# K's tail weights first, a later second output projection, an earlier last w2 piece and earlier weight sums in a pre-LN attention and MLP kernel

## The chip, the cores and the metric

The kernel runs on one core of one Trainium2 chip. The metric is the time of one execution on the device, in microseconds (us). Before the change the median of three runs was 367.53 us (367.42 to 367.68).

The engines are named as in the profile: PE is TensorE, DVE is VectorE, ACT is ScalarE, POOL is GpSimd, and SP is the engine that issues most transfers. "Before" and "after" are the two kernels.

## The reference

One pre-LN transformer block on x of shape (1, 2048, 576), bf16. There are 32 heads of 18 channels. Each position looks at 8 positions, itself and seven earlier ones at distances of 2.

```python
def _A_ref(x, wqkv, wo):                       # sliding, dilated attention
    qkv = (x @ wqkv).reshape(B, S, 3, H, Dh)...             # H = 32, Dh = 18
    idx = pos[:, None] - (jnp.arange(8) * 2)[None, :]       # W = 8, dil = 2
    kg, vg = k[:, :, idx_c, :]..., v[:, :, idx_c, :]...
    logits = einsum("bhsd,bhswd->bhsw", q, kg) * Dh ** -0.5  # masked where idx < 0
    o = einsum("bhsw,bhswd->bhsd", softmax(logits), vg)
    return o.transpose(...).reshape(B, S, D) @ wo

def _B_ref(x, w1, b1, w2, b2):                 # D = 576, F = 4608
    h = _gelu(einsum("bsd,df->bsf", _layernorm(x), w1) + b1)
    return einsum("bsf,fd->bsd", h, w2) + b2

h  = x + _A_ref(_layernorm(x), wqkv, wo)       # first LayerNorm: LN1
h2 = h + _B_ref(_layernorm(h), w1, b1, w2, b2) # second LayerNorm: LN2
```

## The kernel before

The 2048 positions are 16 tiles of 128 rows. `EVEN` and `ODD` list the even and the odd tiles. The program has two stages:

1. Until 69 us it makes Q, K and V, two (tile, part) pairs at a time. One such pair of pairs is a "visit". A visit has two phases, one for each half of the PE's rows. VectorE does the attention of the first tiles meanwhile.
2. From 69 us the tiles go through the MLP in 8 groups of two. While PE does the MLP of one group, VectorE does the attention of later tiles, PE the output projection (`pw`) of the next group's tiles c and d, and ScalarE their LN2. The normalised tiles reach the next MLP through DRAM, by a transposing transfer into `hnT`. Groups 1 and 2 (`k` = 0 and 1) use plain products with w2 (`po`, L576). Groups 3 to 8 use a scheme with fewer products (L661), which needs sums of weights (`w2_sums`) and sums of hidden values (`h_sums`) from VectorE.

The end of the channel dimension, 576 = 4 x 128 + 64, has its own small weight tile `wqh_sb`, the "tail". A "halo" is the copy of a K or V tile, shifted by one row, that is written to DRAM and read back into `kv_ring`. The main queue, issued by SP, carries nearly all loads. Loads issued after the first evacuation are paced: each waits for an evacuation by ScalarE.

The start, in program order:

```python
load_x(EVEN[0:1])
load_x(EVEN[1:2])                    # the second x tile is second on the main queue
load_wqkv(1, 0, 2)                   # t = 1 is K
load_wqkv(1, 2, KF)
load_wqkv_half((nc.scalar, nc.scalar), slice(1, 3))   # tails of K and V, ScalarE's queue
load_x(EVEN[2:3])
...
ln1_even(0)                          # VectorE: statistics and centring of x tile 0
ln1_even_act(1)                      # ScalarE: statistics of x tile 1; VectorE centres it
...
tr_x(EVEN[0:1], "D")                 # PE transposes; the copy into xnT is ScalarE's
tr_x(EVEN[1:2], "C")                 # ... and this copy VectorE's
ln1_even_rstd(0, 1)
ln1_even(2)
for qd in range(len(seq) // 2):      # the visits
    ...
```

The attention of one tile j, the exp, and the two-tile LN2:

```python
def att_pv_a(j):                     # needs the V halo in v_ring
    nc.vector.tensor_tensor(out=prod..., in0=v_ring..., in1=a..., op=ALU.mult)

def pv_t(j):
    pv(j)                            # den, probs, att_pv_a, att_pv_b, next halo read
    dma_tr_o(j)                      # transposed output oT through DRAM

def exps(*js):
    att_exp(*js)                     # ScalarE; loads exp's table
    gelu_table()                     # loads Gelu's table back

def ln2_pair(c, d, js=()):
    ln2_stats(c, d)
    if js:
        att_den(*js)
        att_pv_sum(js[0])
    ln2_send(c); ln2_send(d); ln2_ins(c, d)
    ...
```

Group 1 (`k == 0`; `m1[v]` is what VectorE and SP do ahead of visit v of the MLP's first half, `ia[f]` ahead of row f of its second half; one row is two `po` matmuls):

```python
m1[0] += [c_(halos, 1), c_(att_qk_a, d), c_(att_qk_rest, d, 1), c_(halo, d, 1)]
m1[1] = [c_(pv_t, c), c_(pv_t, d), c_(load_w2, 4), c_(att_qk, e, 0)]
late_wo = wo_duo(c, "B")             # projection of c
ia[12] = [c_(exps, e), lambda d=d: wo_visit((d, "A"), fill=True),   # projection of d
          c_(ln2_pair, c, d, (e,)), c_(halos, 2), c_(send_o, e)]
...
# groups 3 and 4 (k = 2, 3), ahead of visit 3
m1[3] += [c_(w2_sums, *((0, 8) if k == 2 else (8, 12)))]
m1[3] += [c_(h_sums, 0, rows, early)]
```

## Time and profile before

| what | number | view |
|---|---|---|
| median of 3 runs | 367.53 us | times |
| span of the profiled execution | 366.1 us | page |
| PE busy | 358.8 us, 98% | page |
| DVE busy | 299.8 us, 82%; hardly idle from 18 to 186 us | page, slices |
| ACT busy | 231.6 us, 63% | page |
| waits of PE in the middle of the program | 1.35 us at 92.19, 0.37 us at 208.30 | waits, timeline |

The profiled execution took 368.01 us. The page's busy lines and its chain:

```profile
span 366.1 us, 11432 instructions
PE 358.8 (98%) x4899; PEld 292.4 (80%) x4899; DVE 299.8 (82%) x425; ACT 231.6 (63%) x511; POOL 40.9 (11%) x47
...
PE 72%; DVE 18%; DMA 5%; issue 2%; POOL 1%; ACT 0%; ACTq 0%; SPq 0%; POOLq 0%; DVEq 0%
```

The last line says that the chain which ended last consists of PE work for 72% of the span. What PE waited for is in the waits view; its columns are the total, the number of waits, and the longest, in us:

```profile
PE pw L217 <- DMA oT<-td: 1.3, 1, 1.3
PE busy L770 <- PEq L1050: 0.8, 1, 0.8
PE pq L217 <- DMA wq_sb<-in_A_wqkv_dram: 0.6, 2, 0.4
PE po L661 <- DVE kv_ring L641: 0.4, 1, 0.4
PE pq L217 <- ACT q_all L312: 0.2, 1, 0.2
```

These waits add up to 2.5 us, without the one of `busy` at the program's start. The change goes for them. PE's timeline at the start (start, duration, engine, line, operation, and the idle time before it in brackets):

```profile
5.51 0.45 PE L184 MATMUL xt_pt<-ident,q_all 128*128 128x128 bf16 x5
6.30 0.42 PE L217 MATMUL pq<-wq_sb,xnT 64*128 64x288 bf16 x4 [0.17 <-DMA wq_sb<-in_A_wqkv_dram]
7.11 0.42 PE L217 MATMUL pq<-wq_sb,xnT 64*128 64x288 bf16 x4 [0.38 <-DMA wq_sb<-in_A_wqkv_dram]
8.09 1.97 PE L217 MATMUL pq<-wq_sb,xnT 64*128 64x288 bf16 x24
```

Line one is the transposes of the second x tile; the visits begin at 6.30 and wait twice for K weights; the second phase of the first visit begins at 8.09. Later lines of the same view, in groups 1, 2 and 4:

```profile
92.19 0.66 PE L217 MATMUL pw<-wo_sb,oT 64*128 64x288 bf16 x8 [1.35 <-DMA oT<-td]
108.42 0.61 PE L217 MATMUL pm<-hnT,w_sb 64*128 64x256 bf16 x8
208.30 1.64 PE L661 MATMUL po<-q_all,kv_ring 128*128 128x288 f16 x12 [0.37 <-DVE kv_ring L641]
```

And VectorE's timeline where it has time to spare in groups 3 and 4:

```profile
166.97 1.42 DVE L461 TENSOR_TENSOR h<-pw,x_all 128x576 f32<-128x576 f32 x2 [0.64 <-PE pw L217]
189.06 2.56 DVE L397 TENSOR_TENSOR prod<-kv_ring,probs 128x4608 bf16<-128x4608 bf16 x1 [2.50 <-DMA kv_ring<-kv_dram]
```

### The profile page before, as it was taken

What the parts mean: (1) busy time and instruction counts of PE and PEld (TensorE: products, weight loads), DVE (VectorE), ACT (ScalarE), POOL (GpSimd) and SP (SyncE); (2) the same over time, 40 slices, a digit from 0 to 9 for tenths busy, and PEclk for the clock granted to TensorE, in tenths of its full rate; (3) what the DMA queues carried; (4) which work ended last, traced back from release to release, by engine and by line L of the source; (5) the groups of instructions that cost most, each with busy time, mean ns of one, the idle gap of its engine ahead of it and who ended that gap; (6) DMA issues with size and microseconds to landing.
All of it is one profiled execution on the core that took longest, in us unless ns stands there. A gap on an engine that the chain in (4) does not pass through costs nothing.

```text
span 366.1 us, 11432 instructions
## 1 busy us (share of the span) xinstructions
PE 358.8 (98%) x4899; PEld 292.4 (80%) x4899; DVE 299.8 (82%) x425; ACT 231.6 (63%) x511; POOL 40.9 (11%) x47
## 2 busy tenths in 40 slices
PE   8999999999999999999999999999999999999995
PEld 5689877887678877887788778877887788778874
DVE  4899999999999999999969998999994599720331
ACT  4788856798638773568556764686568656616620
POOL 2232004000220031003100021010101010100000
PEclk9999999999999999999999999999999999999999
DMA  8969798953558715510553036304520442030001
GB/s 248 312 177 325 172 213 230 328 194 71 179 143 164 255 60 107 128 41 34 139 102 71 33 92 132 88 32 104 119 72 33 90 85 56 3 90 18 2 2 33
DMA packets 61875, 43.70 MB, mean 119 GB/s; under 512 B 31856, under 2 KB 60144, under 8 KB 61824
## 3 DMA queue, kind: packets, MB, share of 16 engines
q1 hardware_dynamic: 59808, 41.05, 40.7%
q0 software_dynamic: 1728, 1.77, 4.7%
q8 instruction: 38, 0.62, 0.7%
q10 hardware_dynamic: 288, 0.15, 0.2%
q14 instruction: 13, 0.11, 0.1%
HBM read 21.10 MB, written 12.42 MB: 92 GB/s over the span
## 4 chain that ended last, share of the span: by engine, by line
PE 72%; DVE 18%; DMA 5%; issue 2%; POOL 1%; ACT 0%; ACTq 0%; SPq 0%; POOLq 0%; DVEq 0%
PE pm L217 29%; PE po L661 21%; PE po L576 9%; PE pq L217 9%; PE pw L217 4%; DVE prod L397 3%; DVE prod L351 3%; DVE prod L345 2%; DVE prod L403 2%; DMA kv_ring<-kv_dram 2%; DVE ln_stats L151 2%; DMA x_all<-in_A_x_dram 1%; DMA wqh_sb<-in_A_wqkv_dram 1%; DVE kv_ring L641 1%; POOL ln_rstd L164 1%
## 5 line engine op out<-in xcount | busy, mean ns | idle before, releaser
L557 ACT ACTIVATE h_all<-pm,b_sb 128x256 f16<-128x256 f32 (+1 forms) x288 | 108.3, 496 | 70.6 <-PE pm L217 70.6
L217 PE MATMUL pm<-hnT,w_sb 64*128 64x256 bf16 x2304 | 143.0, 269 | 0.0
L217 PEld LDWEIGHTS <-w_sb 64*128 64x128 bf16 x2304 | 111.7, 94 | 15.0 <-issue 1.7
L661 PEld LDWEIGHTS <-h_all 128*128 128x128 f16 x544 | 52.3, 98 | 15.3 <-issue 2.5
L217 PE MATMUL pq<-wq_sb,xnT 64*128 64x288 bf16 x768 | 54.6, 283 | 0.9 <-DMA wq_sb<-in_A_wqkv_dram 0.6
L217 PEld LDWEIGHTS <-xnT 64*128 64x128 bf16 x864 | 43.7, 94 | 10.1 <-issue 1.1
L351 DVE TENSOR_TENSOR prod<-prod 128x2304 bf16<-128x2304 bf16 (+1 forms) x64 | 44.2, 691 | 2.1
L397 DVE TENSOR_TENSOR prod<-kv_ring,probs 128x4608 bf16<-128x4608 bf16 x16 | 40.9, 2556 | 3.9 <-DMA kv_ring<-kv_dram 3.6
L661 PE MATMUL po<-w2a_sb,h_all 128*128 128x288 bf16 (+1 forms) x312 | 43.6, 286 | 0.0
L345 DVE TENSOR_TENSOR prod<-kv_ring,q_all 128x4608 bf16<-128x4608 bf16 x16 | 40.8, 2550 | 0.2
L217 PE MATMUL pm<-hnT,w1h_sb 64*128 64x256 bf16 x288 | 39.2, 269 | 0.0
L481 POOL TENSOR_TENSOR ln_rstd<-ln_var,mhalf 128x1 f32<-128x1 f32 x13 | 15.9, 1220 | 181.5 <-ACT ln_var L480 181.5
L403 DVE TENSOR_TENSOR prod<-prod 128x2304 bf16<-128x2304 bf16 (+1 forms) x32 | 33.8, 1057 | 1.0
L576 PEld LDWEIGHTS <-h_all 128*128 128x128 bf16 x288 | 27.9, 98 | 7.9 <-issue 0.9
L661 PEld LDWEIGHTS <-kv_ring 128*128 128x128 f16 x240 | 23.4, 98 | 6.5 <-DVE kv_ring L641 0.7
L576 PE MATMUL po<-w2a_sb,h_all 128*128 128x288 bf16 x224 | 28.5, 286 | 0.0
L661 PE MATMUL po<-w2b_sb,h_all 128*128 128x288 bf16 (+1 forms) x152 | 22.2, 286 | 0.0
L217 PE MATMUL pw<-wo_sb,oT 64*128 64x288 bf16 x256 | 19.5, 283 | 1.3 <-DMA oT<-td 1.3
L641 DVE TENSOR_TENSOR kv_ring<-h_all 128x1536 f16<-128x1536 f16 (+3 forms) x10 | 6.9, 687 | 15.9 <-ACT h_all L557 15.9
L164 POOL TENSOR_TENSOR ln_rstd<-ln_veps,mhalf 128x1 f32<-128x1 f32 (+2 forms) x14 | 13.5, 971 | 49.3 <-DVE ln_veps L158 34.1
L217 PEld LDWEIGHTS <-oT 64*128 64x128 bf16 x288 | 13.4, 94 | 6.3 <-DMA oT<-td 1.7
L730 ACT COPY po<-po 128x288 f32<-128x288 f32 x18 | 6.9, 385 | 14.6 <-PE po L661 11.4
(107 smaller groups left out, 382.1 us busy)
## 6 DMA issues: line engine op xcount, KB each, us to landing
w_sb<-in_B_w_dram SPq DMA_DIRECT2D x6, 768.0 KB, 5.9
kv_ring<-kv_dram SPq DMA_DIRECT2D x28, 144.0 KB, 2.7
w2a_sb<-in_B_w_dram SPq DMA_DIRECT2D x4, 1008.0 KB, 6.8
kv_dram<-kv_ring SPq DMA_DIRECT2D x13, 288.0 KB, 4.2
out_dram<-o_sb SPq DMA_DIRECT2D x15, 144.0 KB, 3.0
td<-q_all SPq DMA_DIRECT2D x14, 144.0 KB, 2.2
td<-hn SPq DMA_DIRECT2D x14, 144.0 KB, 1.8
x_all<-in_A_x_dram SPq DMA_DIRECT2D x12, 144.0 KB, 2.6
```

Source lines behind the costliest of these rows:

```text
L151: nc.vector.bn_stats(out=stats[:, i, c, :], in_=src[:, c * HALF:(c + 1) * HALF])
L164: nc.gpsimd.tensor_tensor(out=rstd[:], in0=veps[:], in1=mhalf[:].to_broadcast([P, n]), op=ALU.pow)
L217: last = nc.tensor.matmul(duo["g"][r ^ swap][i], lhsT=lhsT, rhs=rhs, start=(swap == 0 and i == 0 and kt == 0), stop=(swap == 1 and kt == K ...
L345: nc.vector.tensor_tensor(out=prod[:], in0=k_ring[j % 2], in1=q_all[:, j, :].unsqueeze(1) .to_broadcast([P, W, D]), op=ALU.mult)
L351: nc.vector.tensor_tensor(out=prod[:, :, o * H:o * H + n], in0=prod[:, :, a * H:a * H + n], in1=prod[:, :, c * H:c * H + n], op=ALU.add)
L397: nc.vector.tensor_tensor(out=prod[:].rearrange("p w (d h) -> p w d h", h=H), in0=v_ring[j % 2].rearrange("p w (d h) -> p w d h", h=H), in ...
L403: nc.vector.tensor_tensor(out=prod[:, 0:n, :], in0=prod[:, 0:n, :], in1=prod[:, n:2 * n, :], op=ALU.add)
L481: nc.gpsimd.tensor_tensor(out=rstd[:], in0=var[:], in1=mhalf[:], op=ALU.pow)
L557: pace[0] = nc.scalar.activation(out=hT(grp)[:, f, 0:N], in_=ps[:, r, i * N:(i + 1) * N], func=ACT.Gelu_apprx_tanh, bias=b1_sb[:, f:f + 1] ...
L576: nc.tensor.matmul(banks[half], lhsT=hT(grp)[:, f, i * P:(i + 1) * P], rhs=w2_rows(f)[:, half * HALF:(half + 1) * HALF], start=(f == 0), s ...
L641: nc.vector.tensor_tensor(out=s_slot(t, m0, m1), in0=a, in1=b, op=alu)
L661: nc.tensor.matmul(bank, lhsT=l, rhs=r, start=start, stop=stop, skip_group_check=True)
```

## The change

It has five parts. I give them names that the rest uses.

- START: the tail weights are split by part, K's are issued first, on ScalarE's queue, with the second x tile between their two halves. VectorE takes the statistics of the third x tile before it copies the second `xnT`. The `ln1_veps` tile has 8 buffers, not 2.
- ACTS: one LN1 tile on ScalarE comes one visit later, behind an evacuation.
- W2: the last piece of w2 (1152 KB, `w2b_sb`) is issued near the start of group 1, not after the attention of its tiles.
- ROWS: the second projection of group 1 moves from row 12 to row 19, the exp of tile e with it. LN2 of tile c goes ahead of it, LN2 of d behind it.
- SUMS: weight sums of group 4 open the group, where VectorE waits 2.50 us for a halo.

Its intent is to take away each of PE's waits in the list above. The diff, with cuts:

```diff
-    def load_wqkv_half(engines, ts):
...
+    def load_wqkv_half(engine, t, r):                                # START
+        c0 = t * D + r * HALF
+        engine.dma_start(out=wqh_sb[half_rows(r), t, :], in_=A_wqkv[KF * P:D, c0:c0 + HALF])
...
         load_x(EVEN[0:1])
-        load_x(EVEN[1:2])
+        for r in range(2):
+            load_wqkv_half(nc.scalar, 1, r)
+            if r == 0:
+                nc.scalar.dma_start(out=x_all[:, EVEN[1], :], in_=x3[:, EVEN[1], :])
         load_wqkv(1, 0, 2)
         load_wqkv(1, 2, KF)
-        load_wqkv_half((nc.scalar, nc.scalar), slice(1, 3))
...
+        for r in range(2):
+            load_wqkv_half(nc.sync, 2, r)                            # and Q's likewise
...
-name="ln1_veps", bufs=2)
+name="ln1_veps", bufs=8)
...
+        ln1_even_stats(2)
         tr_x(EVEN[0:1], "D")
         tr_x(EVEN[1:2], "C")
+        ln1_even_center(2)
         ln1_even_rstd(0, 1)
-        ln1_even(2)
...
-            4: [c_(ln1_rstd, 8), c_(ln1_stats, 9, c_(ln1_bias, 8)), c_(ln1_act, 8, 0), c_(ln1_stats, 10)],
-            5: [c_(ln1_act, 8, 1), ...],
+            4: [c_(ln1_rstd, 8), c_(ln1_stats, 9, c_(ln1_bias, 8)), c_(ln1_stats, 10)],
+            5: [c_(ln1_act, 8, 0), c_(ln1_act, 8, 1), ...],          # ACTS
...
-                m1[0] += [c_(halos, 1), c_(att_qk_a, d), c_(att_qk_rest, d, 1), c_(halo, d, 1)]
+                m1[0] += [c_(halos, 1), c_(load_w2, 4), c_(att_qk_a, d), ...]   # W2
-                m1[1] = [c_(pv_t, c), c_(pv_t, d), c_(load_w2, 4), c_(att_qk, e, 0)]
+                m1[1] = [c_(pv_t, c), c_(pv_t, d), c_(att_qk_a, e), c_(halo, e, 1)]
-                ia[12] = [c_(exps, e), lambda d=d: wo_visit((d, "A"), fill=True), c_(ln2_pair, c, d, (e,)), ...]
+                ia[0] = [c_(ln2_h, c), c_(ln2_act, c), c_(put_b2, c), c_(ln2_send, c), c_(att_qk_rest, e, 0)]
+                ia[19] = [c_(exps, e), lambda d=d: wo_visit((d, "A"), fill=True), c_(ln2_h, d), c_(ln2_act, d),
+                          c_(put_b2, d), c_(att_pv, e), c_(ln2_send, d), c_(ln2_ins, c, d), ...]   # ROWS
...
+                if k == 3:
+                    m1[0] += [c_(w2_sums, 8, 12)]                    # SUMS
...
-                if k in (2, 3):
-                    m1[3] += [c_(w2_sums, *((0, 8) if k == 2 else (8, 12)))]
+                if k == 2:
+                    m1[3] += [c_(w2_sums, 0, 8)]
```

More of the change, by code (lines that the diff above doesn't have):

```diff
@@ L114, in load_wqkv @@
              A_wqkv[k0 * P:k1 * P, t * D:(t + 1) * D].rearrange("(k p) c -> p k c", p=P))
-    def load_wqkv_half(engines, ts):
-        src = A_wqkv[KF * P:D, :].rearrange("p (t g c) -> p t g c", t=3, g=2)
-        for r in range(2):
-            engines[r].dma_start(out=wqh_sb[half_rows(r), ts, :], in_=src[:, ts, r, :])
+    def load_wqkv_half(engine, t, r):
+        c0 = t * D + r * HALF
+        engine.dma_start(out=wqh_sb[half_rows(r), t, :], in_=A_wqkv[KF * P:D, c0:c0 + HALF])
     def load_wo(qs):
@@ L759 @@
         load_wqkv(0)
-        load_wqkv_half((nc.sync, nc.sync), slice(0, 1))
+        for r in range(2):
+            load_wqkv_half(nc.sync, 0, r)
         load_x(ODD[4:8])
@@ L792, in center, with ln1_even_stats, ln1_even_center @@
                                         scalar1=mean, scalar2=None, op0=op)
+        def ln1_even_stats(gi):
+            ln1[gi] = ln_stats([x_all[:, EVEN[gi], :]], f"ln1_{gi}", 1.0, EPS, 1, None, False)
+        def ln1_even_center(gi):
+            center(EVEN[gi], ln1[gi][0][:, 0, 0:1], ALU.subtract)
         def ln1_even(gi):
-            mv, veps = ln1[gi] = ln_stats([x_all[:, EVEN[gi], :]], f"ln1_{gi}", 1.0, EPS, 1, None, False)
-            center(EVEN[gi], mv[:, 0, 0:1], ALU.subtract)
+            ln1_even_stats(gi)
+            ln1_even_center(gi)
         def ln1_even_act(gi):
@@ L809, in ln1_even_rstd @@
                 mv, var = ln1.pop(gi)
-                veps = qp.tile([P, 1], F32, tag="ln1_veps", name="ln1_veps", bufs=2)
+                veps = qp.tile([P, 1], F32, tag="ln1_veps", name="ln1_veps", bufs=8)
                 nc.vector.tensor_scalar(out=veps[:], in0=var[:] if mv is None else mv[:, 0, 1:2],
@@ L862, in ln2_ins, with ln2_pair @@
                     accumulate_h(j)
-        def ln2_pair(c, d, js=()):
+        def ln2_pair(c, d):
             ln2_stats(c, d)
-            if js:
-                att_den(*js)
-                att_pv_sum(js[0])
             ln2_send(c)
@@ L871, in ln2_pair @@
             ln2_ins(c, d)
-            if js:
-                halo(js[0], 2)
         loads = {v: [c_(load_w1, c)] for c, v in enumerate((3, 4, 9, 14, 16, 18))}
@@ L882 @@
             3: [c_(ln1_even_rstd, 6, 7), c_(ln1_stats, 8)],
-            4: [c_(ln1_rstd, 8), c_(ln1_stats, 9, c_(ln1_bias, 8)), c_(ln1_act, 8, 0), c_(ln1_stats, 10)],
-            5: [c_(ln1_act, 8, 1), c_(out_x, 0), c_(ln1_rstd, 9), c_(ln1_bias, 9), c_(att_qk_a, A[0])],
+            4: [c_(ln1_rstd, 8), c_(ln1_stats, 9, c_(ln1_bias, 8)), c_(ln1_stats, 10)],
+            5: [c_(ln1_act, 8, 0), c_(ln1_act, 8, 1), c_(out_x, 0), c_(ln1_rstd, 9), c_(ln1_bias, 9), c_(att_qk_a, A[0])],
             6: [c_(ln1_rstd, 10), c_(ln1_act, 8, 2), c_(halo, A[0], 1)],
@@ L973 @@
             if k == 0:
-                m1[0] += [c_(halos, 1), c_(att_qk_a, d), c_(att_qk_rest, d, 1), c_(halo, d, 1)]
+                m1[0] += [c_(halos, 1), c_(load_w2, 4), c_(att_qk_a, d), c_(att_qk_rest, d, 1), c_(halo, d, 1)]
                 mid[0] = {1: [c_(exps, d)]}
-                m1[1] = [c_(pv_t, c), c_(pv_t, d), c_(load_w2, 4), c_(att_qk, e, 0)]
+                m1[1] = [c_(pv_t, c), c_(pv_t, d), c_(att_qk_a, e), c_(halo, e, 1)]
                 late_wo = wo_duo(c, "B")
-                ia[12] = [c_(exps, e), lambda d=d: wo_visit((d, "A"), fill=True), c_(ln2_pair, c, d, (e,)), c_(halos, 2), c_(send_o, e)]
+                ia[0] = [c_(ln2_h, c), c_(ln2_act, c), c_(put_b2, c), c_(ln2_send, c), c_(att_qk_rest, e, 0)]
+                ia[19] = [c_(exps, e), lambda d=d: wo_visit((d, "A"), fill=True), c_(ln2_h, d), c_(ln2_act, d), c_(put_b2, d),
+                          c_(att_pv, e), c_(ln2_send, d), c_(ln2_ins, c, d), c_(halo, e, 2), c_(halos, 2), c_(send_o, e)]
                 ib[0] = [c_(finish_out, g[0])]
```

## The prediction

> **What bounds it.** TensorE. The page gives PE 98% of the 366.1 us span at full clock; the chain of waits is PE for 72%, DVE for 18%. The waits view and PE's timeline show about 3.3 us of real stalls; nothing else can be won:
> - 0.17 + 0.38 us for K weights (`wq_sb`) at 6.3 and 7.1, about 0.4 us for V weights before 9.87;
> - 0.36 us at 24.87, where ScalarE stood on `ln_nmr`, then ran an LN1 tile before the evacuation;
> - 1.35 us at 92.19: the second output projection in group 1, waiting for its `oT` transfer;
> - 0.4 us near 208: `po` waiting for `kv_ring` (h sums, L641).
>
> VectorE hardly idles from 18 to 186.
>
> **Start.** Half of the tail weights leaves the K path: K 0.5 us sooner. But VectorE now runs the statistics of the third x tile ahead of the copy of the second `xnT`. They need that tile landed: 7.49 us before, by estimate 6.0 to 6.8 now. Then come 1.04 us of statistics, 0.49 of copy, 0.37 of centring, 0.2 for `ln_veps`, and 1.08 on Pool for two `ln_rstd`, behind which stand Pool's end-of-phase markers. So the first visit's second phase starts near 9.3 to 10.1 us, not 8.09. The V stall vanishes; net +0.7 to +1.6 us on PE. More `ln_veps` buffers take away two VectorE waits (0.60 + 0.36 at 17 us). Moving the LN1 tile removes most of the 0.36. PE is then 0.9 us late until 90 us; the old wait absorbs it.
>
> **Group 1.** The second projection goes from row 12 to row 19: 7 x 0.245 = 1.7 us of `po` work, enough to cover 1.35. But:
> - The last w2 piece (1.18 MB; at the trace's 352 GB/s 3.3 us) joins a queue that drained at 78.8 us. The Trainium skill ("DMA: Bandwidth & Descriptors", Queues, rings and completion order) says descriptors are consumed in ring order, so the halo read issued at 77.9 (landed 79.93) should land near 82.5, after VectorE wants it (81.0 to 81.9), and the first `oT` about 0.7 us later.
> - The transposed `hnT` landed at 107.98; the next MLP began at 108.42. With LN2 apart, ScalarE does tile c, the exp table load (1.28 us, as the skill's "ScalarE: Activation LUTs", What ACT_TABLE_LOAD costs, says), exp, the Gelu load, then tile d: by the durations from 94 to 103 us, d is sent at about the old time.
>
> So the next MLP starts -0.5 to +0.2 us against 108.42, not -1.4. VectorE waits 1 us more for exp, perhaps 0.1 us of PE in group 3.
>
> **Group 4.** The weight sums (4 x 0.76 us) move into VectorE's 2.50 us of idle time at 186.5. The h sums end about 2.5 us sooner and the stall at 208 goes: -0.5.
>
> **Sum.** -0.2, +0.1, -0.5: about -0.6. Predicted **366.8 us, 365.2 to 368.3** (8 in 10). Faster by over 2%: 0.02; within 2%: 0.96; slower: 0.02.
>
> **Right or wrong, seen in:** PE's timeline (second phase from 9.3 to 10.1; no `pw` wait near 92; `pm` of group 2 at 107.9 to 108.6, just after `hnT`; no stall near 208); the DMA landings (halo near 82.5); VectorE's waits (none at 186.5).
>
> **What would make it wrong:** x landing by 5.5 us, so that the start gains; no delay of the halo, so that group 1 gains all 1.4 us (then 365.5); VectorE falling behind in groups 2 and 3 (then 368).

## The result, and the profile after

| | median | runs |
|---|---|---|
| before, same chip | 367.48 us | 366.89 to 367.68, 4 runs |
| after | 369.11 us | 368.93 to 370.33, 4 runs |

The ratio is 1.0054 (95% interval 1.003 to 1.0079). Ratios here are the mean time of one kernel's fast runs over that of the other's of the same rounds, so they are not quite the ratios of the medians. The change costs about half a per cent. It is within 2%, but above the predicted range.

The page after. The span is 0.7 us longer than that of before, against 1.6 us between the medians, partly because the profiled execution of before (368.01 us) was a slow one:

```profile
span 366.8 us, 11434 instructions
PE 360.5 (98%) x4899; PEld 294.6 (80%) x4899; DVE 299.3 (82%) x425; ACT 231.4 (63%) x511; POOL 39.7 (11%) x47
...
PE 67%; DVE 25%; DMA 4%; issue 2%; ACT 1%; POOL 1%; ACTq 0%; DVEq 0%; POOLq 0%
```

The chain holds more DVE (25%, was 18%). PE's waits after:

```profile
PE pm L215 <- DVE prod L349: 0.8, 1, 0.8
PE busy L773 <- PEq L1059: 0.8, 1, 0.8
PE xt_pt L182 <- DVE q_all L790: 0.7, 1, 0.7
PE pq L215 <- ACT kv_ring L310: 0.3, 1, 0.3
```

The waits for `oT`, for `wq_sb`, and for `kv_ring` at 208 are gone from the list. The wait behind an evacuation by ScalarE only moved: 0.20 us at 24.87 before, 0.30 us at 28.76, one visit later, now. Two others are new. The first is put down to DVE's `prod`, which these matmuls don't read. The weight loads in front of them name the true releaser:

```profile
109.57 0.36 PEld L215 LDWEIGHTS <-w_sb 64*128 64x128 bf16 x8 [1.12 <-DMA hnT<-td]
```

The transfer of `hnT` landed at 109.46 in the trace, and the MLP began 0.14 us later, as it did after the landing in e1 and e14 below. The start:

```profile
6.64 0.71 PE L182 MATMUL xt_pt<-ident,q_all 128*128 128x128 bf16 x5 [0.67 <-DVE q_all L790]
7.54 1.14 PE L215 MATMUL pq<-wq_sb,xnT 64*128 64x288 bf16 x8
9.91 1.73 PE L215 MATMUL pq<-wq_sb,xnT 64*128 64x288 bf16 x24
12.26 0.66 PE L215 MATMUL pq<-wq_sb,xnT 64*128 64x288 bf16 x8
```

The second x tile is transposed 1.13 us later than before, and slower: 0.71 us for the five matmuls that took 0.45. The next group is 8 matmuls in 1.14 us, where 8 of the same kind take 0.66 us at 12.26, in the last line. These are the two speeds of PE's clock. Groups 1, 2 and 4:

```profile
94.18 0.54 PE L215 MATMUL pw<-wo_sb,oT 64*128 64x288 bf16 x6
109.60 0.61 PE L215 MATMUL pm<-hnT,w_sb 64*128 64x256 bf16 x8 [0.84 <-DVE prod L349]
209.49 1.63 PE L659 MATMUL po<-q_all,kv_ring 128*128 128x288 f16 x12
```

VectorE in group 1:

```profile
83.96 2.56 DVE L395 TENSOR_TENSOR prod<-kv_ring,probs 128x4608 bf16<-128x4608 bf16 x1 [1.51 <-DMA kv_ring<-kv_dram]
98.30 0.60 DVE L389 TENSOR_REDUCE den<-logits 128x32 f32<-128x256 f32 x1 [0.61 <-ACT logits L381]
```

Both waits are new. The first is the halo that queues behind the w2 piece: it landed at 83.87, not 79.93. The second is exp. In before, ScalarE loaded exp's table at 89.50, while it stood idle, and exp began at 94.48. In after the load runs from 96.56 to 97.84, behind the LN2 of tile c, so its 1.28 us lie on VectorE's way.

Where PE stood at each milestone, from the starts of its matmuls in the two traces:

| milestone | before | after | difference |
|---|---|---|---|
| second phase of the first visit | 8.09 | 9.91 | +1.83 |
| visit 5 begins | 19.48 | 21.07 | +1.58 |
| MLP of group 1 begins | 68.85 | 70.53 | +1.68 |
| MLP of group 2 | 108.42 | 109.60 | +1.17 |
| MLP of group 3 | 146.17 | 147.34 | +1.18 |
| MLP of group 4 | 183.14 | 184.86 | +1.72 |
| MLP of group 5 | 220.17 | 221.35 | +1.18 |
| last matmul starts | 362.00 | 363.18 | +1.18 |

So the start loses 1.6 us. The late projection's wait of 1.35 us is gone, but the wait of 0.84 us for `hnT` comes instead. Group 3 loses 0.54 us. Group 4 wins 0.54 us, against an execution of before that had a stall there.

### The profile page after: what moved, and what is told of

It is laid out like the page before. It is cut to its first block, busy times and chain, and to the rows that moved or that the text cites. A ratio compares the mean times of both kernels' runs of the same rounds, so it can differ in the third digit from the quotient of the medians.

```text
span 366.8 us, 11434 instructions
## 1 busy us (share of the span) xinstructions
PE 360.5 (98%) x4899; PEld 294.6 (80%) x4899; DVE 299.3 (82%) x425; ACT 231.4 (63%) x511; POOL 39.7 (11%) x47
## 3 DMA queue, kind: packets, MB, share of 16 engines
q0 software_dynamic: 1728, 1.77, 4.6%
## 4 chain that ended last, share of the span: by engine, by line
PE 67%; DVE 25%; DMA 4%; issue 2%; ACT 1%; POOL 1%; ACTq 0%; DVEq 0%; POOLq 0%
PE pm L215 30%; PE po L659 25%; DVE prod L349 5%; PE po L574 5%; DVE prod L343 5%; DVE prod L395 4%; PE pq L215 3%; PE pw L215 3%; DVE prod L401 3%; DMA kv_ring<-kv_dram 1%; DVE peak L362 1%; DMA x_all<-in_A_x_dram 1%; DMA x_all<-b_bc 1%; DVE ln_stats L149 1%; DVE h L459 1%
## 5 line engine op out<-in xcount | busy, mean ns | idle before, releaser
L215 PEld LDWEIGHTS <-w_sb 64*128 64x128 bf16 x2304 | 113.3, 94 | 14.5 <-issue 1.4
L215 PE MATMUL pq<-wq_sb,xnT 64*128 64x288 bf16 x768 | 55.4, 286 | 0.3 <-ACT kv_ring L310 0.3
L479 POOL TENSOR_TENSOR ln_rstd<-ln_var,mhalf 128x1 f32<-128x1 f32 x13 | 14.6, 1123 | 183.4 <-ACT ln_var L478 183.4
```

Source lines behind the costliest of these rows:

```text
L215: last = nc.tensor.matmul(duo["g"][r ^ swap][i], lhsT=lhsT, rhs=rhs, start=(swap == 0 and i == 0 and kt == 0), stop=(swap == 1 and kt == K ...
L479: nc.gpsimd.tensor_tensor(out=rstd[:], in0=var[:], in1=mhalf[:], op=ALU.pow)
```

## Experiments

All kernels gave correct results. Each was timed in 5 rounds against before on the same chip. PE's times below are those of the one profiled execution, against the trace of before; positive is later. The executions of one kernel scatter by 1 us and more, so a trace shows a mechanism, and the ratio decides about the time.

| run | what | median, us | before | ratio (95%) |
|---|---|---|---|---|
| e1_nostart | after, START undone | 367.74 | 367.47 | 1.0007 (0.9995 to 1.0019) |
| e2_w2late | after, W2 undone | 370.33 | 367.47 | 1.0075 (1.0063 to 1.0087) |
| e3_only_start | before, START alone | 368.53 | 367.47 | 1.0044 (1.0021 to 1.0066) |
| e4_only_sums | before, SUMS alone | 367.39 | 367.47 | 0.9998 (0.9986 to 1.0011) |
| e5_x1_second | after, second x tile back on the main queue | 368.52 | 367.42 | 1.0038 (1.0013 to 1.0063) |
| e6_stats_later | after, early statistics undone | 370.12 | 367.42 | 1.0066 (1.004 to 1.0092) |
| e7_filler | after, five more matmuls keep PE busy | 369.00 | 367.42 | 1.0053 (1.0032 to 1.0074) |
| e8_before_again | before, as a control | 367.48 | 367.42 | 1.0012 (0.9988 to 1.0037) |
| e9_rows_only | before, ROWS alone | 368.53 | 367.46 | 1.0026 (1.0008 to 1.0043) |
| e10_w2_only | before, W2 alone | 367.76 | 367.46 | 1.0016 (1.0003 to 1.0029) |
| e11_k_split | before, K's tails split and first | 366.96 | 367.46 | 0.9991 (0.9979 to 1.0003) |
| e12_row19 | before, projection at row 19, exp stays | 368.35 | 367.46 | 1.0025 (1.0013 to 1.0037) |
| e13_changed_start_mended | after, e5 and e6 together | 368.17 | 367.81 | 1.0008 (0.9989 to 1.0027) |
| e14_row19_w2_early | e12 with W2 | 368.70 | 367.81 | 1.0028 (1.0003 to 1.0052) |
| e15_w2_between | e11 and e12, w2 between the two tiles | 370.19 | 367.81 | 1.0068 (1.0048 to 1.0088) |
| e16_w2_between_sums | e15 with SUMS | 368.71 | 367.81 | 1.0026 (1.0004 to 1.0048) |
| e17_k_split_sums | e11 with SUMS | 367.29 | 367.52 | 0.9994 (0.9981 to 1.0008) |

### Which part costs it: e1 to e4

The theory was that the start loses what the traces show. The rival was that the early w2 piece, through the halo, is the cost.

e1_nostart takes START out of after:

```diff
-        for r in range(2):
-            load_wqkv_half(nc.scalar, 1, r)
-            if r == 0:
-                nc.scalar.dma_start(out=x_all[:, EVEN[1], :], in_=x3[:, EVEN[1], :])
+        load_x(EVEN[1:2])
...
-        ln1_even_stats(2)
         tr_x(EVEN[0:1], "D")
...
+        ln1_even(2)
```

> The changed kernel with its start undone (load order, order of the statistics, ln_veps buffers as before); all else stays. Theory 1 (the start costs 1.6 us, and the waits that should have absorbed it moved along with it): the first visit's second phase is back at 8.1 us, the MLP of group 2 starts within 0.3 us of 108.4 (changed kernel: 109.6), time 0.999 to 1.000 of before. Rival A (the last w2 piece issued early is the whole loss, by the halo read it holds up): still 1.003 or more. Rival B (the PE clock was released late by chance of the execution): the release time in the trace has nothing to do with which kernel runs.

The ratio fell from 1.0054 to 1.0007. In the trace the second phase began at 7.54 and the MLP of group 2 at 107.57 (-0.86), sooner than I had expected. So START is nearly the whole cost. What was gained by then went in group 3, where PE waited 1.02 us for the h sums:

```profile
169.33 0.78 PE L661 MATMUL po<-w2b_sb,h_all 128*128 128x288 bf16 x5
171.12 1.15 PE L661 MATMUL po<-q_all,kv_ring 128*128 128x288 f16 x8 [1.02 <-DVE kv_ring L641]
```

e2_w2late puts the w2 piece back:

```diff
-                m1[0] += [c_(halos, 1), c_(load_w2, 4), c_(att_qk_a, d), ...]
-                m1[1] = [c_(pv_t, c), c_(pv_t, d), c_(att_qk_a, e), c_(halo, e, 1)]
+                m1[0] += [c_(halos, 1), c_(att_qk_a, d), ...]
+                m1[1] = [c_(pv_t, c), c_(pv_t, d), c_(load_w2, 4), c_(att_qk_a, e), c_(halo, e, 1)]
```

> The changed kernel with the last w2 piece issued where it was (behind the second attention tile of group 1). Theory 1: the halo read lands before VectorE wants it, so VectorE's 1.5 us wait near 82 goes; the MLP of group 2 starts near 108.7 instead of 109.6, because PE itself is 1.68 us late by then; group 3 has no stall of 0.5 us; time 0.999 to 1.001 of before. Rival A: the whole loss goes and the MLP of group 2 starts before 108.0: time 0.997 or less.

It was not faster, 1.0075 against 1.0054 (the intervals overlap), where 0.999 to 1.001 was expected. VectorE's wait at 82 was gone, but the piece landed at 99.27 and PE waited 0.74 us for it. The early w2 is therefore not what makes after slow. With a later projection the late piece makes PE wait.

e3_only_start is before with START alone:

```diff
+ (the lines that e1 takes out, put into before)
```

> The kernel before with the new start alone. Theory 1: first visit's second phase near 9.9 us, PE 1.6 us late at the fourth visit; the old wait for the second projection at 92.19 shrinks, so that the MLP of group 2 starts only about 0.6 us later than 108.4; time 1.001 to 1.003 of before. If the start alone costs as much as the whole change (1.005), nothing absorbed it.

The ratio was 1.0044, above the expected 1.001 to 1.003. PE waited 2.21 us for the second x tile and lost its clock:

```profile
4.79 0.44 PE L182 MATMUL xt_pt<-ident,q_all 128*128 128x128 bf16 x5
5.16 0.24 PE L186 MATMUL xt_pt<-ident,q_all 128*64 128x128 bf16 x1
7.62 0.71 PE L182 MATMUL xt_pt<-ident,q_all 128*128 128x128 bf16 x5 [2.21 <-DVE q_all L790]
8.26 0.32 PE L186 MATMUL xt_pt<-ident,q_all 128*64 128x128 bf16 x1
```

The clock is read from stretches of the same trace. The columns are the window, its length, the busy time and number of instructions of PE, weight loads, DVE, ACT and POOL, then the granted clock, the DMA share and GB/s:

```profile
4.30:7.60 3.30, 0.95 (x12) 0.57 (x9) 0.66 (x3) 1.19 (x3) 0.00 (x0) 1.00 1.04 346
7.70:11.00 3.30, 3.30 (x28) 2.05 (x30) 3.02 (x12) 0.99 (x4) 1.08 (x2) 0.50 0.74 210
11.10:14.50 3.40, 3.40 (x50) 2.23 (x46) 3.26 (x13) 2.06 (x3) 0.31 (x1) 1.00 1.03 323
```

PE was busy for 0.95 of 3.3 us, and in the next 3.4 us it ran at half clock: 28 matmuls, where the stretch after has 50. The Trainium skill ("TensorE: Matmul & The Clock Gate", What's actually happening) says that the clock follows PE's activity in free-running windows of 3413 ns. That agrees: all stretches of half clock in the middle of these runs lasted 3.41 or 3.42 us.

This run also tests whether the old wait for `oT` absorbs a late start, since its projection stands at row 12 as in before:

```profile
93.67 0.66 PE L215 MATMUL pw<-wo_sb,oT 64*128 64x288 bf16 x8 [0.64 <-DMA oT<-td]
```

It hardly does. `oT` landed at 93.62, not 92.15, so PE still waited 0.64 us there. PE was 2.18 us late at the MLP of group 1 and still 1.77 us late at that of group 2.

e4_only_sums is before with SUMS alone:

```diff
+                if k == 3:
+                    m1[0] += [c_(w2_sums, 8, 12)]
...
-                    m1[3] += [c_(w2_sums, *((0, 8) if k == 2 else (8, 12)))]
+                    m1[3] += [c_(w2_sums, 0, 8)]        # for k == 2 only
```

> The kernel before with the weight sums of group 4 moved to its opening, alone. They run in VectorE's idle time near 186.5 to 189; the stall of 0.53 us near 208 goes and nothing else changes: 0.9985 of before, PE ends about 0.5 us sooner. If no gain: the moved sums only shifted the wait.

The stall at 208 was gone, and the MLP of group 5 began 0.66 us sooner than in the trace of before. The time did not move: 0.9998. Why, e8 shows.

### The two steps of the start: e5 to e8

The theory now had two steps. (a) The second x tile lands later, behind a weight load on ScalarE's queue, so PE idles and loses its clock. (b) VectorE works in order, so the early statistics, which wait for the third x tile, hold up the second `xnT` copy.

e5_x1_second takes (a) away and keeps (b):

```diff
+        load_x(EVEN[1:2])
         for r in range(2):
             load_wqkv_half(nc.scalar, 1, r)
-            if r == 0:
-                nc.scalar.dma_start(out=x_all[:, EVEN[1], :], in_=x3[:, EVEN[1], :])
```

> The changed kernel with the second x tile back as the second load of the main queue (the K tail weights stay split, the statistics stay early). Theory S (the early statistics of the third tile hold up Pool's phase markers): the second phase of the first visit still starts at 9.3 to 9.8 us and the fourth visit is still 1.0 to 1.3 us later than before. Theory C (the second x tile, behind a weight load on ScalarE's queue, lands at 5.4 to 6.5 us; PE idles and its granted clock is at half until 10 or 11 us): second x tile lands near 4.2 us, the clock is granted in full from 5 us at the latest and stays, the fourth visit is within 0.5 us of before's.

The second x tile landed at 3.61, not 5.38, and the clock was full from 4.63 us. Step (b) then stands alone:

```profile
7.11 0.82 DVE L149 BATCH_NORM_STATS2 ln_stats<-x_all 128x6 f32<-128x288 bf16 x2 [2.25 <-DMA x_all<-in_A_x_dram]
7.96 0.21 DVE L150 BATCH_NORM_AGGREGATE ln_mv<-ln_stats 128x2 f32<-128x12 f32 x1
8.09 0.44 DVE L270 COPY xnT<-xt_pt 128x640 bf16<-128x640 bf16 x1
```

VectorE waited 2.25 us for the third x tile and only then copied the second. On PE:

```profile
8.58 0.66 PE L215 MATMUL pq<-wq_sb,xnT 64*128 64x288 bf16 x8 [1.33 <-DVE xnT L270]
```

Visit 5 began 0.78 us later than before. The ratio was 1.0038 (1.0013 to 1.0063), against 1.0008 (0.9989 to 1.0027) with neither step (e13 below). The delay by step (b) is plain in the trace, but what it costs in time is not settled: these intervals overlap, and the two slowest of the six executions (369.89 and 370.53 us) are also the two with a mean clock of 0.995. GpSimd was in `ln_rstd` from 8.95 to 10.03 while the second phase began at 9.21. GpSimd's markers (empty instructions by which the program tells PE that a phase is over) were therefore not what held PE, as the prediction had thought. The profile's spans of GpSimd are rough, but PE shows no wait in front of that phase either.

e6_stats_later takes (b) away and keeps (a):

```diff
-        ln1_even_stats(2)
         tr_x(EVEN[0:1], "D")
         tr_x(EVEN[1:2], "C")
-        ln1_even_center(2)
         ln1_even_rstd(0, 1)
+        ln1_even(2)
```

> The changed kernel with the statistics of the third x tile back behind the copy of the second xnT (loads as changed). Theory S: the second phase of the first visit starts near 8.1 to 8.8 us and most of the 1.6 us is gone. Theory C: PE still idles until the second x tile has landed, the clock is still at half until 10 us or later, the second phase starts at 9.5 us or later and the fourth visit is still over 1.2 us late.

The second x tile landed at 6.00, PE waited 1.46 us, the clock fell to half from 8.80 to 12.22, and visit 5 began 2.63 us late. Ratio 1.0066 (1.004 to 1.0092), clear of e13's interval: step (a) costs by itself.

e7_filler keeps START and gives PE five more matmuls while it waits:

```diff
         tr_x(EVEN[0:1], "D")
+        fill = psum_pair("B", "fill")
+        for _ in range(5):
+            nc.tensor.matmul(fill[:, 0, 0:512], lhsT=ones[:, 0:P], rhs=ones[:], start=True, stop=True)
         tr_x(EVEN[1:2], "C")
```

> The changed kernel with five matmuls of 512 columns (their result is not used) between the transposes of the first and of the second x tile, to keep PE busy there. Theory C, clock part: the clock is granted in full from 5 us and stays, transposes of the second tile take 0.45 instead of 0.7 us; fourth visit 0.2 to 1.2 us sooner than in the changed kernel. If PE is gated by Pool's markers (theory S), the clock is full but the fourth visit moves by 0.3 us at most.

The clock was full from 3.40 us, although the second x tile landed at 5.82. None of its 6 executions had a mean clock of 0.995 or less, against 2 of 4 of after, 4 of 6 of e3 and 3 of 6 of e6. Visit 5 began 0.80 us sooner than in after. This supports that the clock was lost because PE idled; six executions are few, and a mean clock can't show a late first grant (see e14). But the ratio, 1.0053, is that of after. In the trace the gain was gone by the MLP of group 2 (109.47, against 109.60): PE waited 1.27 us for `oT`, until 94.95, because that transfer took 4.24 us to land, where it took 2.67 to 2.91 us in all other traces. So no run shows that the clock alone cost time.

e8_before_again is before, unchanged:

```diff
  (no edit)
```

> The kernel before, unchanged, as a control: ratio 1.000 within 0.15%. Its trace tells how much of the stalls at 92 and 208 us is of every execution: if the stall of 0.5 us at 208 is absent here, the gain from the weight sums was predicted from a stall of one execution, which would explain why they gave 0.0002 alone.

The ratio, 1.0012 (0.9988 to 1.0037), shows the resolution of such a comparison. Its profiled execution was its slowest (370.26 us), and even so the stall of group 4 isn't there:

```profile
209.56 1.14 PE L661 MATMUL po<-w2b_sb,h_all 128*128 128x288 bf16 x8
210.54 1.63 PE L661 MATMUL po<-q_all,kv_ring 128*128 128x288 f16 x12
```

Six traces without SUMS (e3, e8, e10, e11, e12, e15) have no stall there, and in e9 and e14 group 4 took only about 0.1 us longer. The cause is a transfer: the halo that VectorE waits for near 189 took 5.91 us to land in the trace of before, 3.81 in e8 and 3.76 in e10, and VectorE's wait of 2.50 us was 0.41 and 0.33 us there. The 0.5 us that the prediction counted were in the one profiled execution of before and not in the typical one.

### Group 1, part by part: e9 to e12

e9_rows_only is before with ROWS alone. The w2 piece stays behind `pv_t(d)`.

```diff
-                m1[1] = [c_(pv_t, c), c_(pv_t, d), c_(load_w2, 4), c_(att_qk, e, 0)]
+                m1[1] = [c_(pv_t, c), c_(pv_t, d), c_(load_w2, 4), c_(att_qk_a, e), c_(halo, e, 1)]
...
-                ia[12] = [c_(exps, e), lambda d=d: wo_visit((d, "A"), fill=True), c_(ln2_pair, c, d, (e,)), ...]
+                ia[0] = [c_(ln2_h, c), c_(ln2_act, c), c_(put_b2, c), c_(ln2_send, c), c_(att_qk_rest, e, 0)]
+                ia[19] = [c_(exps, e), lambda d=d: wo_visit((d, "A"), fill=True), c_(ln2_h, d), ...]
```

> The kernel before with the second projection at row 19 and LN2 of its two tiles apart, as in the change; the last w2 piece, the start and the sums as before. Theory V (in the changed order VectorE waits 0.6 us for exp, because ScalarE now does LN2 of the first tile and two table loads ahead of it; it enters group 3 late and PE then waits for its h sums): the wait of 0.6 us before the softmax denominators near 95.7 is there, none near 82; PE gains up to 0.4 us by the MLP of group 2 and gives 0.5 us or more back at about 170 us; ratio 1.000 to 1.002. Rival W (the early w2 piece is what makes VectorE late): no stall near 170, ratio 0.998 to 0.999.

The wait for `oT` was gone and the MLP of group 2 began at 107.23, which is 1.20 us sooner than before. So the intended mechanism works in this trace. PE waited 0.33 us for the w2 piece, VectorE 0.60 us for exp. This was the fastest execution of the kernel, 366.87 us. The other five took 367.92 to 369.36, and the ratio is 1.0026. What the slower ones lost isn't seen in a trace.

e10_w2_only is before with W2 alone:

```diff
-                m1[0] += [c_(halos, 1), c_(att_qk_a, d), c_(att_qk_rest, d, 1), c_(halo, d, 1)]
-                m1[1] = [c_(pv_t, c), c_(pv_t, d), c_(load_w2, 4), c_(att_qk, e, 0)]
+                m1[0] += [c_(halos, 1), c_(load_w2, 4), c_(att_qk_a, d), c_(att_qk_rest, d, 1), c_(halo, d, 1)]
+                m1[1] = [c_(pv_t, c), c_(pv_t, d), c_(att_qk, e, 0)]
```

> The kernel before with only the last w2 piece issued early. Rival W: the halo read lands near 82.2 us, VectorE waits 0.3 to 0.8 us for it near 82, the first oT of group 1 comes late (PE waits up to 0.5 us near 85), the MLP of group 2 starts 0.3 to 0.8 us later, a stall near 170 follows; ratio 1.001 to 1.002. Theory V: VectorE absorbs it, ratio 1.000.

The halo landed at 82.15, as against the estimate of 82.5 in the prediction. VectorE waited 0.42 us, and PE's wait for `oT` grew to 1.65 us. Ratio 1.0016.

e11_k_split is before with the harmless part of START: K's tails split and first on ScalarE's queue, and the second x tile where it was.

```diff
         load_x(EVEN[1:2])
+        for r in range(2):
+            load_wqkv_half(nc.scalar, 1, r)
         load_wqkv(1, 0, 2)
         load_wqkv(1, 2, KF)
-        load_wqkv_half((nc.scalar, nc.scalar), slice(1, 3))
...                                          # V's and Q's tails split likewise, on the main queue
```

> The kernel before with only the tail weights of K split off and loaded first (second x tile still second on the main queue, statistics in the old order). The useful part of the new start: K's weights land by 6.3 to 6.7 instead of 7.07 us, the clock is full from 5 us, the fourth visit comes 0.3 to 0.8 us sooner; the wait for the second projection keeps part of it; ratio 0.998 to 0.9995.

The ratio, 0.9991, has an interval that includes 1. The start gained nothing in this trace: visit 4 began 0.09 us later than before's, not 0.3 to 0.8 us sooner. The end of the program is shorter instead, by 0.45 us ("What stays open" below).

e12_row19 moves the projection alone. The exp stays at row 12 and LN2 stays in one piece.

```diff
-                ia[12] = [c_(exps, e), lambda d=d: wo_visit((d, "A"), fill=True), c_(ln2_pair, c, d, (e,)), ...]
+                ia[12] = [c_(exps, e)]
+                ia[19] = [lambda d=d: wo_visit((d, "A"), fill=True), c_(ln2_pair, c, d, (e,)), ...]
```

> The kernel before with only the second projection moved to row 19; exp stays at row 12 and LN2 of both tiles stays together. Theory V: VectorE gets to the residual sum at 94.4 us either way, so it loses nothing; PE's wait of 1.35 us at 92 goes, the MLP of group 2 starts when hnT lands (108.0, so 0.3 to 0.45 us sooner) and no stall comes near 170; ratio 0.9985 to 0.9995. If a stall of 0.5 us near 170 comes here too, VectorE's exp wait isn't its cause.

VectorE had no wait for exp, so that wait comes from moving exp behind tile c's LN2. But the w2 piece, issued at 90.89, landed at 98.67:

```profile
98.71 1.02 PE L576 MATMUL po<-w2b_sb,h_all 128*128 128x288 bf16 x7 [2.14 <-DMA w2b_sb<-in_B_w_dram]
```

A later projection brings the rows of `po` forward. They then reach the last piece of w2 before it is there. The old wait for `oT` had hidden that.

### Mended versions: e13 to e17

e13_changed_start_mended is after with both e5's and e6's edits:

```diff
  (the edits of e5 and e6 together)
```

> The changed kernel with the second x tile back as second load of the main queue and the statistics of the third tile back behind the copy; the K tail weights stay split and first. If the start's loss is those two steps and nothing else: clock full from 6.5 us at the latest in every execution, the fourth visit within 0.3 us of before's or sooner, ratio 0.999 to 1.001 (changed kernel: 1.005). If some other part of the start costs, over 1.002.

The ratio was 1.0008 (0.9989 to 1.0027). The clock was full from 3.73 us. So (a) and (b) together account for START's loss, within these intervals; the split of the tails costs nothing. In its trace the MLP of group 2 began at 108.54 (+0.12), but group 3 lost 1.6 us to h sums.

e14_row19_w2_early is e12 with W2:

```diff
  (the edits of e12 and e10 together)
```

> The kernel before with the second projection at row 19, exp kept at row 12, LN2 together, and the w2 piece early as in the change. Theory V (the wait for exp makes VectorE late for group 3): no wait before the denominators near 95.7, no stall near 170, no stall for w2 near 96; the MLP of group 2 is held by hnT at 108.0 to 108.5; ratio 0.999 to 1.0005. If there is still a stall near 170, the early w2 piece alone is enough for it.

No wait for w2, none for exp, and no stall in group 3. But PE's gain went into the next gate (the next thing that PE has to wait for), the transfer of `hnT`:

```profile
108.62 0.61 PE L217 MATMUL pm<-hnT,w_sb 64*128 64x256 bf16 x8 [1.23 <-DMA hnT<-td]
```

The ratio was 1.0028, above the expected 0.999 to 1.0005, with the profiled execution the fastest of six.

By chance this execution has its clock windows at the same phase as that of after (full clock from 6.68 us here, from 10.10 in after), with the old start. Of e14 first, then of after, in the columns of e3's fence:

```profile
3.30:6.60 3.30, 3.15 (x20) 1.84 (x18) 1.50 (x5) 2.39 (x7) 0.00 (x0) 1.00 0.98 300
6.70:10.00 3.30, 3.28 (x49) 2.20 (x49) 2.99 (x11) 1.25 (x3) 1.08 (x2) 1.00 1.06 348
```

```profile
3.30:6.60 3.30, 2.52 (x14) 1.35 (x12) 1.55 (x6) 1.63 (x4) 0.00 (x0) 1.00 1.03 335
6.70:10.00 3.30, 3.30 (x28) 2.10 (x30) 3.02 (x11) 1.02 (x4) 1.08 (x2) 1.00 0.98 271
```

PE was busy for 3.15 us of the first window in one and 2.52 us in the other. In the next window it did 49 matmuls in one and 28 in the other. The granted clock reads 1.00 in all four lines, because the first clock record of after's trace comes at 10.10 us. The half clock shows only in the durations.

e15_w2_between puts the w2 piece between the attention of the two tiles, with e11's and e12's edits:

```diff
-                m1[1] = [c_(pv_t, c), c_(pv_t, d), c_(load_w2, 4), c_(att_qk, e, 0)]
+                m1[1] = [c_(pv_t, c), c_(load_w2, 4), c_(pv_t, d), c_(att_qk, e, 0)]
```

> A mended version: K tail weights split and first, second projection at row 19 with exp at row 12, w2 piece issued between the two attention tiles of group 1 (behind the halo read and the first oT). The halo read lands near 80, w2 by 90, PE waits neither at 92 nor at 96; the MLP of group 2 starts with hnT near 107.5 to 108; ratio 0.997 to 0.999 (beats both kernels).

Now the piece stood ahead of tile d's own transfers, and the projection waited even at row 19:

```profile
96.02 0.66 PE L215 MATMUL pw<-wo_sb,oT 64*128 64x288 bf16 x8 [2.10 <-DMA oT<-td]
```

Ratio 1.0068, where 0.997 to 0.999 was expected: it is a bad place.

e16_w2_between_sums adds SUMS to it:

```diff
+                if k == 3:
+                    m1[0] += [c_(w2_sums, 8, 12)]
...
```

> The version with the w2 piece between the two attention tiles, and the weight sums opening group 4 as well. If the sums only help executions in which the halo read at 183 us is slow: within 0.0005 of the same version without them.

Its profiled execution, the slowest of six, has the same wait of about 2.1 us for `oT`. The clock was half from 95.58 to 99.00 behind it. Ratio 1.0026. That e15 and e16 differ by more than SUMS can explain shows how far executions scatter; I draw nothing finer from this pair.

e17_k_split_sums joins the two parts that cost nothing:

```diff
  (the edits of e11 and e4 together)
```

> The two parts of the change that cost nothing alone, on the kernel before: K tail weights split off and first (second x tile second, statistics in the old order), and the weight sums opening group 4. If the parts add: 0.9991 times 0.9998, so about 0.999 of before (367.0 us), never slower; group 1 is as before. If it is above 1.000, the gain of the K split alone was chance.

Ratio 0.9994 (0.9981 to 1.0008). No version that I ran beats before beyond its interval.

### The stall in group 3, added up

PE's stall near 171 us can be followed from VectorE's waits, because VectorE has no other spare time in that stretch. Before has 0.64 us at 166.97 (shown above), and its second h sum ended 1.07 us before PE used it (169.72 and 170.79). Lateness beyond the 0.64 us shows in the h sums, and what then exceeds PE's own lateness plus 1.07 us is a stall. In us, against the trace of before:

| trace | VectorE's waits after 80 us that before has not | its h sums | PE on arrival | sum: h sums - PE - 1.07 | stall, from the starts |
|---|---|---|---|---|---|
| after | 1.51 halo, 0.61 exp, 0.46 halo | +2.47 | +1.18 | 0.22 | 0.27 |
| e1_nostart | 0.81 halo, 0.61 exp, 0.64 and 0.54 halo | +1.35 | -0.85 | 1.13 | 1.18 |
| e9_rows_only | 0.60 exp, 0.41 halo | +0.10 | -1.19 | 0.22 | 0.27 |
| e13_changed_start_mended | 1.44 halo, 0.60 exp, 0.68 and 0.55 halo | +2.49 | +0.12 | 1.30 | 1.35 |
| e14_row19_w2_early | 0.62 and 0.62 halo | +0.40 | +0.20 | -0.87 | none |
| e10_w2_only | 0.42 halo | +0.24 | +0.24 | -1.07 | none |

The stall is the distance between two starts, less the usual one; the waits view counts a little less (1.02 us in e1). A second wait of 0.26 us follows the first in after, e1, e9 and e13, and is not in the table. For after the waits also add up: VectorE was 0.56 us behind at 80 us, waited 1.51 + 0.61 + 0.46 us more, and had 0.64 us to spare. That gives 2.50 us, and the h sums were 2.47 us late. The same sum fits the six other traces that stall there (e2, e5, e6, e7, e15, e16: 1.08, 0.96, 0.30, 0.29, 1.48 and 1.17 by the sum, 1.13, 1.01, 0.36, 0.34, 1.53 and 1.22 measured). So the stall has two causes: new waits of VectorE, for the halo and for exp or a late projection, and a PE that comes sooner. Whatever PE wins in group 1 beyond about 1 us it waits for here.

## Why the prediction was wrong

The class was right: within 2%. The time was wrong: 366.8 us with a range to 368.3 was predicted, and 369.11 us measured. Point by point:

- **"PE is then 0.9 us late until 90 us; the old wait absorbs it."** This is the step that failed. The late start moved PE by 1.58 us at visit 5, not 0.9. And the old wait is not a fixed point in time that PE can be late against. The evacuations that follow PE pace the loads: the w2 load ahead of the halo was issued 1.68 us later than before (71.47, not 69.79) and landed 1.2 us later (78.93, not 77.70). So halo, VectorE, exp and `hnT` came later too, and the MLP of group 2 began at 109.60, not at 107.9 to 108.6. With START undone (e1) `hnT` landed at 107.43, not 109.46. With START alone (e3) the old wait took up only 0.41 of 2.18 us. e1 shows START to be the cost (1.0054 to 1.0007), e3 shows it alone (1.0044).
- **Why START's term was mis-sized.** I counted the third tile's statistics, step (b), which e5 shows alone: +0.78 us at visit 5. I did not count the second x tile, step (a). It landed at 5.38, where ScalarE had begun on it at 4.25 in before, so PE idled and kept half clock until 10.1 us. I had looked only at the third tile, which landed at 6.38, as estimated (6.0 to 6.8). The second phase began at 9.91, inside the predicted 9.3 to 10.1, but partly for that other reason: that hit is in part luck. The Trainium skill ("DMA: Bandwidth & Descriptors", Issuing engines are not separate DMA queues) says that issuing from another engine saves only the time to issue and that the transfers share the same 16 DMA engines. The runs are consistent with that: on ScalarE's queue, behind one half of K's tail, the tile was issued only 0.12 us later than second on the main queue (1.32, e5: 1.20), but it landed at 5.38 to 6.36 (after, e2, e3, e6, e7) and not at 3.61 (e5).
- **"Moving the LN1 tile removes most of the 0.36."** Not so. The view has 0.20 us there, and in all seven kernels with ACTS a wait of about 0.3 us stands one visit later. No run has ACTS alone; it is still in e1 (1.0007) and e13 (1.0008).
- **"Behind which stand Pool's end-of-phase markers."** Not so: in e5 the second phase began at 9.21, while GpSimd was busy from 8.95 to 10.03.
- **The halo behind the w2 piece.** The mechanism was right. With W2 alone it landed at 82.15 (e10; estimate 82.5), as the order of the ring suggests, in the section that the prediction cites. In after it landed at 83.87, because the whole queue ran later.
- **The gain of the later projection, and the next gate.** Right: no wait for `pw` near 92, and PE then met `hnT`. The wait of 1.35 us was worth only what lies between it and the next gate: in before, `hnT` landed at 107.98, 0.44 us ahead of its use. In e14 PE gave 1.23 us of it back there.
- **"VectorE waits 1 us more for exp, perhaps 0.1 us of PE in group 3."** The size was wrong. The exp wait was 0.61 us, but with the two halo waits it was 2.58 us, and PE lost 0.54 us. e14, with exp left at row 12, has no stall; e15 and e16, also with exp there, do have one, because the late projection and the halo hold VectorE up. The table load behind it took 1.28 us, as the skill says ("ScalarE: Activation LUTs", What ACT_TABLE_LOAD costs).
- **"The stall at 208 goes: -0.5."** In the two traces that is what happened (-0.54). But e4 gives 0.9998, and e8 with five other traces has no such stall. A gain was counted from one execution that was slower than the median.

The sum of the prediction was -0.2, +0.1, -0.5 us. The traces have +1.17, +0.54, -0.54 us, and the last is missing in a typical execution of before.

What stays open: one trace is not a distribution, and the slower executions of e9 and e14 are not explained, nor whether e14 (1.0028) really costs more than e1 (1.0007), which has all of the change but START: their intervals overlap. The landing of the w2 piece scatters (5.9 to 7.8 us from issue, where it was issued late) and no run says why.

One small thing the traces do settle: PE's last matmul is 1.18 us later in after, the span only 0.73 us longer. From the end of the last matmul to the end of the span it is 3.79 to 3.82 us in the eight traces without split tails (before, e1, e4, e8, e9, e10, e12, e14) and 3.35 to 3.37 us in the eleven with them. So the split shortens the program's end by 0.45 us, and the 0.0009 of e11 (0.33 us) is no more than that. How the split does it was not tested.

## What to carry to other kernels

Keep what the first matmuls need at the head of the main queue, and put nothing that waits for a later transfer into an in-order engine ahead of work that is needed now: here the two cost about 1.7 us (1.0054 in after, 1.0008 in e13). PE's clock was lost on the way, but the run that kept it (e7) was no faster. A wait is worth only the distance to the next gate, and an engine that is full (VectorE here, with 0.64 + 1.07 us to spare from 80 to 171 us) turns any new wait into a stall further on. Look for a stall in a second execution before you count on its removal.

## What the Trainium skill lacked or had wrong

- "TensorE: Matmul & The Clock Gate", HAM oscillation: the rule there is to avoid PE-idle gaps over about 3.4 us. In these runs single waits of 2.21 us (e3), 1.46 us (e6) and 2.06 us (e16) were followed by a window of half clock, with 2.36, 1.58 and 2.06 us idle in the 3.41 us window before it. Windows with 1.15 us idle (e5) and 0.76 us (e7) kept a clock that was full, but so did windows with 1.60 us (e12, from 94.75) and 1.71 us (e15, from 94.31). For the first grant, 2.52 us busy of 3.3 were too few in after, and 3.15 enough in e14. So gaps far shorter than 3.4 us can cost the clock, but neither the length of one gap nor the idle share of one window sorts all of these cases.
- No page says that a profile's granted clock can be blind at the start; the clock page only warns in general that the clock events of a trace can be unreliable. After's clock reads 1.00 before its first record at 10.10 us, while 8 matmuls took 1.14 us, not 0.66.
- "ScalarE: Activation LUTs", What ACT_TABLE_LOAD costs: beside the load of 1283 ns it counts a drain of 1380 ns. The load agrees (1.28 us), but no drain shows: in after the load began at 96.56 and exp at 97.85.
- "DMA: Bandwidth & Descriptors" gives a figure for memory latency under load, but none for how far the landing of one large transfer scatters. The 1152 KB piece of w2 took 6.1 us from issue to landing in before and 7.8 us in e12, on the same queue at the same place in the program. At the 352 GB/s that the DMA moved from 6 to 14 us in the trace of before, it would be an estimated 3.4 us.
